# Forming the weighted sum of K with K as the weights: a decode block's backward pass on one Trainium2 core

## The chip, the core and the metric

The kernel runs on one core of one Trainium2 chip. The metric is the device time of one execution in microseconds (us), as the median of several runs. A separate execution was recorded by the hardware profiler; its page and trace are what this document reads.

## What is computed

The reference takes one token (a row `x` of 448 values) through a decode block and returns the output together with the gradients of its inputs. The first half is attention with 16 query heads over 8 cached K/V heads of width 256, so that two query heads share each K/V head (a "group", g = 0 to 7). Only the last W = 4096 of the Sk = 32768 cached positions are used. The second half is a gated feed-forward layer of width 1792.

```python
k = k_cache[:, :, Sk - W:, :]          # repeated for the two heads of a group
scores = einsum("bhqd,bhkd->bhqk", q, k) * Dh ** -0.5
p = softmax(scores)
o = einsum("bhqk,bhkd->bhqd", p, v)
h = x + o.reshape(B, Sq, Hq * Dh) @ wo
out = h + ((g * u) @ w_down)           # g, u: layernorm(h) @ w_gate, @ w_up
# returned: out, and the gradients of x, k_cache, v_cache, wq, wo, w_gate, w_up, w_down
```

The gradients of `k_cache` and `v_cache` have the shape of the whole caches. They are zero outside of the window, and those zeros have to be written too: 8 groups x 28672 positions x 256 values x 2 bytes, for each of the two.

For the gradient of the query the kernel needs, for each head, the weighted sum of K, that is the sum over the 4096 positions of p times the row of K. It is called `kbar`. The change concerns how `kbar` is formed.

## The kernel before

**Zeros.** At the start (lines 57 to 62) a tile of zeros is set on VectorE, and SyncE (SP) issues 16 transfers that copy it to the parts of the two cache gradients outside of the window (`out_2`, `out_3`). They are on SP's own DMA queue, and nothing in the kernel waits for them but its end.

**Everything else goes through GpSimd's (POOL's) DMA queue**, in program order: the loads of K and V windows (`load_window`, line 79), of the weights, and all other outputs. Where the tile scheduler finds that a load's target is still being read, the POOL instruction waits, and whatever is behind it on POOL waits too.

**Storage.** `S` holds eight slots of 128 partitions x 8192 values, each wide enough for one window of one group (128 partitions x T = 32 positions x 256). The tables `K_SLOT` and `V_SLOT` (lines 35 and 36) say which group's K and V lie in which slot; slots are used again, so a load has to wait for the last reader of what lay there.

**First half, per group g** (the loop at line 349). The loop issues the loads of the next groups, then `softmax(g)`, then `scores(g + 1)`, then `moments(g)`.

- `scores` (line 279, through `products` at 260) transposes K on TensorE (line 266), copies the transposes out of PSUM alternately on ScalarE (line 210) and VectorE (line 212), and multiplies by the query (line 271).
- `softmax` (line 283) makes the probabilities, once as f32 (`pf`) and once as bf16 (`pT_all`), both laid out as position on partitions, and 32 x 2 columns (t, head).
- `moments` (line 308) goes over the 32 values of t in pairs. For each t and each of the two heads VectorE forms K times the probability into a small buffer `pk` (line 318; three buffers in turn, each for two values of t). Then TensorE issues, for each t: two matmuls of 512 columns into `MT` (line 322, V as weights, both heads' products `pk` as columns), two matmuls of 2 columns into columns 0 to 3 of `acc` (line 325, V as weights, the two heads' probabilities as columns: the attention output), and four matmuls of 1 column into columns 4 to 7 of `acc` (line 329, the products `pk` as weights, a column of ones as the moving operand). The last four add up the products over the 128 partitions: they are `kbar`. The ends of the group copy `MT` and `acc` out (lines 331 to 335).

After the last group `wo` is applied (its second part is loaded at line 376, and line 383 multiplies), followed by the feed-forward layer forward and backward, the gradient of the attention output (line 435) and of the query (line 453, which uses `Mt` and, through line 456, `kbar`).

**Second half, per group** (the loop at line 560): V is transposed again (line 568), the softmax's gradient is formed, and the gradients of the window's K and V are built as matmuls of 512 columns (line 602), copied out of PSUM (lines 210 and 212) into a staging slot and written by POOL at line 607. Outer products for the weights' gradients are formed between them and written at line 477.

The order of instructions on each engine is not written by hand: a scheduler interleaves `scores(g + 1)` with `moments(g)`, and can reorder loads on POOL.

Of the kernel before, what the change touches and what calls it, by code (L numbers as in the profile page):

```python
# [19 lines left out]
T = 32  # L20
# [20 lines left out]
def kernel(  # L41
# [3 lines left out]
    V_, S_, P_ = nc.vector, nc.scalar, nc.tensor  # L45
# [58 lines left out]
    ones_bf = const.tile([128, 128], bf16)  # L104
# [136 lines left out]
    pT_all = const.tile([128, G, T, 2], bf16)  # L241
# [13 lines left out]
    def pk_buf():  # L255
        k = NB + pk_ctr[0] % NB
        pk_ctr[0] += 1
        return Rt[:, k * 1024:(k + 1) * 1024].rearrange("p (i h d) -> p i h d", i=2, h=2)
# [49 lines left out]
    def moments(g):  # L308

        K, Vv, pf = Kw[g], Vw[g], p_f[g]  # L310
        MT = fps.tile([128, 2, 2 * Dh], f32, tag="MT", name="MT")
        acc = fps.tile([128, 8], f32, tag="acc", name="acc")
        for c in range(T // 2):
            pk = pk_buf()
            for i in range(2):
                t = 2 * c + i
                for h in range(2):
                    V_.tensor_scalar(out=pk[:, i, h, :], in0=K[:, t, :], scalar1=pf[:, t, h:h + 1], scalar2=None, op0=ALU.mult)  # L318
            for i in range(2):
                t = 2 * c + i  # L320
                for hf in range(2):
                    P_.matmul(MT[:, hf, :], lhsT=Vv[:, t, hf * 128:(hf + 1) * 128], rhs=pk[:, i, :, :].rearrange("p h d -> p (h d)"),  # L322
                              start=(t == 0), stop=(t == T - 1))
                for hf in range(2):
                    P_.matmul(acc[:, 2 * hf:2 * hf + 2], lhsT=Vv[:, t, hf * 128:(hf + 1) * 128], rhs=pT_all[:, g, t, :],  # L325
                              start=(t == 0 and hf == 0), stop=(t == T - 1), skip_group_check=True)
                for h in range(2):
                    for dk in range(2):
                        P_.matmul(acc[:, 4 + 2 * h + dk:5 + 2 * h + dk], lhsT=pk[:, i, h, dk * 128:(dk + 1) * 128], rhs=ones_bf[:, 0:1],  # L329
                                  start=False, stop=(t == T - 1), skip_group_check=True)  # L330
        S_.copy(out=Mt[:, g, 0, :], in_=MT[:, 0, :])  # L331
        V_.tensor_copy(out=Mt[:, g, 1, :], in_=MT[:, 1, :])
        V_.tensor_copy(out=oT_f[:, 4 * g:4 * g + 4].rearrange("p (h f) -> p f h", f=2), in_=acc[:, 0:4].rearrange("p (f h) -> p f h", h=2))
        V_.tensor_copy(out=kbar[:, 4 * g:4 * g + 4], in_=acc[:, 4:8])
        V_.tensor_copy(out=oT_bf[:, 4 * g:4 * g + 4], in_=oT_f[:, 4 * g:4 * g + 4])
# [13 lines left out]
    for g in range(G):  # L349
        if g + 1 < NV:  # L350
            load_V(g + 1)
        if g + 2 < 7:
            load_K(g + 2)
        if g == 5:
            load_V(5)
        if g == 6:
            load_V(6)
            load_K(7)
        if g == 7:
            load_V(7)  # L360
            IO.dma_start(out=woA, in_=wo_v[:, 0:16, :])
        softmax(g)
        if g + 1 < G and g != 6:
            scores(g + 1)
        moments(g)
        if g == 6:
            scores(7)
        if g == 0:

            t = ps.tile([128, D], f32, tag="tmp", bufs=1)  # L370
            P_.matmul(t[:], lhsT=ones_bf[0:1, :], rhs=go_bf[:], start=True, stop=True)
            S_.copy(out=dh2_bc[:], in_=t[:])
            for c in range(FC):
                V_.tensor_tensor_reduce(out=wd0[:, c, :], in0=wd0[:, c, :], in1=dh2_bc[:], scale=1.0, scalar=0.0,
                                        op0=ALU.mult, op1=ALU.add, accum_out=d_hh[:, c:c + 1])
# [73 lines left out]
    for h in range(H):  # L449
        for dk in range(2):  # L450
            for hf in range(2):
                c0 = (h % 2) * Dh + dk * 128
                P_.matmul(dq_ps[:, 2 * h + dk:2 * h + dk + 1], lhsT=Mt[:, h // 2, hf, c0:c0 + 128], rhs=doT_f[:, 2 * h + hf:2 * h + hf + 1],  # L453
                          start=(hf == 0), stop=(hf == 1))
# [105 lines left out]
    for g in range(G):  # L560
# [3 lines left out]
        for q in range(8):  # L564
# [6 lines left out]
            for i in range(4):  # L571
                for dh in range(2):
                    P_.matmul(dp[:, 4 * q + i, :], lhsT=xt[:, i, dh, :], rhs=doT[:, 4 * g + dh:4 * g + dh + 3:2],  # L573
                              start=(dh == 0), stop=(dh == 1))
# [22 lines left out]
        for c in range(T // 2):  # L597
            d_ps = bps.tile([128, 2, 2, Dh], f32, tag="d2", bufs=2)
            for i in range(2):
                t = 2 * c + i  # L600
                k, a = t // 8, t % 8
                P_.matmul(d_ps[:, i, :, :].rearrange("p w d -> p (w d)"), lhsT=rows[32 * k:32 * k + 32, a, :], rhs=R[32 * k:32 * k + 32, :],  # L602
                          start=True, stop=True)
# [36 lines left out]
```

## Time and profile before

| | us |
|---|---|
| median of the runs (three, 816.27 to 816.81) | 816.36 |
| the profiled execution, its own time | 816.48 |
| its span in the profile | 814.7 |
| TensorE busy, of the span | 504.1 |
| VectorE busy | 374.4 |
| ScalarE busy | 165.0 |

The span runs from the first to the last instruction or transfer that the profiler saw; 1.78 us of the execution's own time lie around it. In the profile PE is TensorE's matmuls, PEld its weight loads, DVE VectorE, ACT ScalarE, POOL GpSimd, SP SyncE; L329 is line 329. `a<-b` in a row is an operation that writes tile a from tile b, followed by partitions x elements and by the count after an x. A strip of 40 digits gives the busy share of 40 equal slices of the span in tenths (9 is 90% or more); "PEclk" is the clock that TensorE was granted, in tenths of full speed. A matmul's duration overlaps its neighbours', so the spacing of their starts says more about TensorE than the duration.

### The profile page before, as it was taken

How to read it: one execution, taken by the hardware profiler on the slowest of the kernel's cores; microseconds unless marked ns; L12 is line 12 of the kernel's file. 1: busy time of each engine (PE TensorE's matmuls, PEld its weight loads, DVE VectorE, ACT ScalarE, POOL GpSimd, SP SyncE). 2: the span in 40 equal slices, each digit the busy share in tenths (PEclk: the TensorE clock that was granted, in tenths of full speed). 3: DMA queues.
4: the chain of work that ended last, by engine and by line, in shares of the span. 5: the costliest groups of instructions: out<-in, count | busy, mean ns of one | idle time of the engine just before them, and what ended most of it. 6: DMA issues, size and time to landing. Idle time of an engine off the chain costs nothing.

```text
span 814.7 us, 12155 instructions
## 1 busy us (share of the span) xinstructions
PE 504.1 (62%) x4991; PEld 301.7 (37%) x4991; DVE 374.4 (46%) x1149; ACT 165.0 (20%) x261; POOL 40.4 (5%) x75
## 2 busy tenths in 40 slices
PE   3559969999566947062995562597597848263200
PEld 3445646666434524031983421243143313010000
DVE  4128837776451644028733470754553626253200
ACT  0230211221101000001012231243343424142100
POOL 3000000000000001000001000001000010000000
PEclk9959878999785969565556555555555555555555
DMA  8999999999999999999999999999999999999993
GB/s 344 430 423 427 430 428 429 425 428 426 430 417 426 415 424 420 428 429 431 426 427 429 409 415 421 431 423 422 404 430 425 425 413 423 421 425 427 424 427 170
DMA packets 24573, 338.66 MB, mean 416 GB/s; under 512 B 1251, under 2 KB 1317, under 8 KB 4677
## 3 DMA queue, kind: packets, MB, share of 16 engines
q1 hardware_dynamic: 14596, 234.88, 68.3%
q0 software_dynamic: 9920, 103.00, 30.2%
q8 instruction: 39, 0.64, 0.3%
q14 instruction: 18, 0.14, 0.0%
HBM read 57.28 MB, written 280.59 MB: 415 GB/s over the span
## 4 chain that ended last, share of the span: by engine, by line
issue 59%; DMA 17%; PE 11%; DVE 4%; POOL 3%; ACT 1%; POOLq 0%; DVEq 0%
DMA S<-in_A_wo_dram 4%; DMA Rt<-in_A_wq_dram 4%; DMA out_dram<-Mt 3%; PE dq_ps L453 3%; DMA S<-in_A_k_cache_dram 3%; DMA S<-in_A_v_cache_dram 2%; PE MT L322 2%; POOL out_dram L477 1%; POOL S L79 1%; DVE Rt L423 1%; POOL out_dram L607 1%; PE dh_ps L159 1%; PE d_ps L602 1%; PE tr L568 1%; PE t L413 1%
## 5 line engine op out<-in xcount | busy, mean ns | idle before, releaser
L602 PE MATMUL d_ps<-R,Mt 32*128 32x512 bf16 x256 | 124.4, 612 | 94.4 <-DVE S L212 93.6
L322 PE MATMUL MT<-Rt,S 128*128 128x512 bf16 x512 | 156.8, 391 | 21.1 <-DMA S<-in_A_v_cache_dram 19.9
L318 DVE TENSOR_SCALAR Rt<-S,pf 128x256 bf16<-128x256 bf16 x512 | 117.8, 283 | 32.0 <-PE acc L329 17.3
L212 DVE CAST S<-d_ps 128x512 bf16<-128x512 f32 x128 | 86.8, 689 | 57.1 <-ACT S L210 43.9
L210 ACT CAST S<-d_ps 128x512 bf16<-128x512 f32 x128 | 75.1, 587 | 171.6 <-PE d_ps L602 171.6
L266 PE MATMUL tr<-ident_bf,S 128*128 128x128 bf16 x512 | 52.5, 267 | 44.5 <-DMA S<-in_A_k_cache_dram 41.2
L602 PEld LDWEIGHTS <-Mt 32*128 32x128 bf16 x256 | 23.2, 113 | 148.1 <-issue 146.7
L325 PEld LDWEIGHTS <-S 128*128 128x128 bf16 x512 | 49.9, 98 | 62.7 <-issue 6.6
L568 PE MATMUL tr<-ident_bf,S 128*128 128x128 bf16 x512 | 68.8, 304 | 3.5 <-ACT Mt L210 3.5
L329 PE MATMUL acc<-ones_bf,Rt 128*128 128x1 bf16 x1024 | 61.8, 163 | 0.0
L568 PEld LDWEIGHTS <-S 128*128 128x128 bf16 x512 | 48.5, 135 | 28.0 <-issue 27.8
L266 PEld LDWEIGHTS <-S 128*128 128x128 bf16 x512 | 41.4, 121 | 42.9 <-DMA S<-in_A_k_cache_dram 41.7
L210 ACT COPY Rt<-tr 128x1024 bf16<-128x1024 bf16 x32 | 32.4, 1012 | 84.7 <-PE tr L266 84.3
L325 PE MATMUL acc<-pT_all,S 128*128 128x2 bf16 x512 | 49.1, 165 | 0.0
L329 PEld LDWEIGHTS <-Rt 128*128 128x128 bf16 x1024 | 44.5, 96 | 0.0
L212 DVE COPY Rt<-tr 128x1024 bf16<-128x1024 bf16 x32 | 22.1, 690 | 48.5 <-PE tr L266 47.0
L210 ACT COPY Mt<-tr 128x1024 bf16<-128x1024 bf16 x32 | 32.4, 1014 | 56.3 <-PE tr L568 29.2
L322 PEld LDWEIGHTS <-S 128*128 128x128 bf16 x512 | 32.0, 97 | 21.7 <-DMA S<-in_A_v_cache_dram 20.4
L331 ACT COPY Mt<-MT 128x512 f32<-128x512 f32 x8 | 4.7, 586 | 164.8 <-PE MT L322 145.4
L573 PEld LDWEIGHTS <-Mt 128*128 128x128 bf16 x512 | 19.9, 108 | 36.7 <-DVE Mt L212 13.7
L573 PE MATMUL dp<-doT,Mt 128*128 128x2 bf16 x512 | 22.6, 168 | 12.3 <-DVE Mt L212 10.5
L212 DVE COPY Mt<-tr 128x1024 bf16<-128x1024 bf16 x32 | 22.0, 686 | 16.4 <-PE tr L568 11.3
(182 smaller groups left out, 435.1 us busy)
## 6 DMA issues: line engine op xcount, KB each, us to landing
out_dram<-zeros SPq DMA_DIRECT2D x16, 14336.0 KB, 149.7
out_dram<-S POOLq DMA_DIRECT2D x16, 2048.0 KB, 29.5
S<-in_A_v_cache_dram POOLq DMA_DIRECT2D x11, 2048.0 KB, 35.6
S<-in_A_k_cache_dram POOLq DMA_DIRECT2D x8, 2048.0 KB, 28.0
out_dram<-Mt POOLq DMA_DIRECT2D x6, 896.0 KB, 22.3
S<-in_A_wq_dram POOLq DMA_DIRECT2D x1, 3584.0 KB, 14.7
S<-in_A_wo_dram POOLq DMA_DIRECT2D x2, 1792.0 KB, 35.4
out_dram<-Mt POOLq DMA_DIRECT2D x3, 1024.0 KB, 35.7
```

Of the source, the lines that this page charges most:

```text
L79: IO.dma_start(out=dst, in_=cache[0, g, Sk - W:, :].rearrange("(p t) d -> p t d", t=T))
L210: S_.copy(out=out, in_=in_)
L212: V_.tensor_copy(out=out, in_=in_)
L266: P_.transpose(tr[:, i, dh, :], Xw[:, 4 * q + i, dh * 128:(dh + 1) * 128], ident_bf[:])
L318: V_.tensor_scalar(out=pk[:, i, h, :], in0=K[:, t, :], scalar1=pf[:, t, h:h + 1], scalar2=None, op0=ALU.mult)
L322: P_.matmul(MT[:, hf, :], lhsT=Vv[:, t, hf * 128:(hf + 1) * 128], rhs=pk[:, i, :, :].rearrange("p h d -> p (h d)"), start=(t == 0), stop=( ...
L325: P_.matmul(acc[:, 2 * hf:2 * hf + 2], lhsT=Vv[:, t, hf * 128:(hf + 1) * 128], rhs=pT_all[:, g, t, :], start=(t == 0 and hf == 0), stop=(t ...
L329: P_.matmul(acc[:, 4 + 2 * h + dk:5 + 2 * h + dk], lhsT=pk[:, i, h, dk * 128:(dk + 1) * 128], rhs=ones_bf[:, 0:1], start=False, stop=(t == ...
L453: P_.matmul(dq_ps[:, 2 * h + dk:2 * h + dk + 1], lhsT=Mt[:, h // 2, hf, c0:c0 + 128], rhs=doT_f[:, 2 * h + hf:2 * h + hf + 1], start=(hf = ...
L568: P_.transpose(tr[:, i, dh, :], Vw[g][:, 4 * q + i, dh * 128:(dh + 1) * 128], ident_bf[:])
L573: P_.matmul(dp[:, 4 * q + i, :], lhsT=xt[:, i, dh, :], rhs=doT[:, 4 * g + dh:4 * g + dh + 3:2], start=(dh == 0), stop=(dh == 1))
L602: P_.matmul(d_ps[:, i, :, :].rearrange("p w d -> p (w d)"), lhsT=rows[32 * k:32 * k + 32, a, :], rhs=R[32 * k:32 * k + 32, :], start=True, ...
```

## The change

The four matmuls of 1 column become two of 2 columns. The weights are now K's own tile (128 positions x 128 of the 256 columns) instead of the product `pk`, and the moving operand is the two heads' bf16 probabilities instead of a column of ones. The same four columns of `acc` receive the result: columns 4 + dk and 6 + dk.

```diff
@@ moments(g), for each t @@
-                for h in range(2):
-                    for dk in range(2):
-                        P_.matmul(acc[:, 4 + 2 * h + dk:5 + 2 * h + dk], lhsT=pk[:, i, h, dk * 128:(dk + 1) * 128], rhs=ones_bf[:, 0:1],
-                                  start=False, stop=(t == T - 1), skip_group_check=True)
+                for dk in range(2):
+                    P_.matmul(acc[:, 4 + dk:7 + dk:2], lhsT=K[:, t, dk * 128:(dk + 1) * 128], rhs=pT_all[:, g, t, :],
+                              start=False, stop=(t == T - 1), skip_group_check=True)
```

The products `pk` stay: line 322 still needs them. TensorE becomes a reader of K's slot within `moments`, which it was not before.

Over the kernel, 8 groups x 32 values of t x 4 = 1024 matmuls and their weight loads become 512 and 512. On POOL the scheduler puts some loads in another order: for the last groups it issues V6, K7, the first part of `wo`, V7 where it issued K7, V6, V7, the first part of `wo`.

## The prediction, as it was put on record

> **What bounds the kernel now.** I read the page's strips first, since a kernel that writes so much may be held by its transfers.
>
> ```profile
> PE   3559969999566947062995562597597848263200
> PEclk9959878999785969565556555555555555555555
> DMA  8999999999999999999999999999999999999993
> GB/s 344 430 423 427 430 428 429 425 428 426 430 417 426 415 424 420 428 429 431 426 427 429 409 415 421 431 423 422 404 430 425 425 413 423 421 425 427 424 427 170
> DMA packets 24573, 338.66 MB, mean 416 GB/s; under 512 B 1251, under 2 KB 1317, under 8 KB 4677
> ## 3 DMA queue, kind: packets, MB, share of 16 engines
> q1 hardware_dynamic: 14596, 234.88, 68.3%
> q0 software_dynamic: 9920, 103.00, 30.2%
> q8 instruction: 39, 0.64, 0.3%
> ```
>
> The DMA strip is 9 in all slices but the first and the last: the 16 DMA engines have work without a break. TensorE's strip falls to 0 in places, and to 0 at the end. The bytes are set by the outputs: the zeros (SP's queue, q1) are 234.88 MB, POOL's queue (q0) carries 103.00 MB. The slices between the ends move 404 to 431 GB/s; 338.66 MB at 425 are 797 us. So the transfers alone explain the span but for some 18 us at its two ends (814.7 - 797).
>
> Next the end, by windows (columns: PE, PEld, DVE, ACT, POOL busy with counts, PE's clock, DMA share, GB/s), POOL's last instructions, and what was issued there.
>
> ```profile
> 765.00:797.00 32.00, 0.00 (x0) 0.00 (x0) 0.00 (x0) 0.00 (x0) 0.00 (x0) 0.50 1.01 430
> 797.00:815.00 18.00, 0.00 (x0) 0.00 (x0) 0.00 (x0) 0.00 (x0) 0.00 (x0) 0.50 0.30 127
> ```
> ```profile
> 761.91 0.53 POOL L607 DMA_DIRECT2D out_dram<-S  x1 [0.19 <-issue]
> ```
> ```profile
> L607 POOL DMA_DIRECT2D out_dram<-S x16: 532/533/589, 517.1 to 761.9; - x16
> DMA to landing us min/median/max: 17.0/29.5/41.4
> ```
>
> No compute engine does anything after 765, and yet 50 us follow with transfers, 32 of them at full rate. The last output is issued at 761.9; with the longest landing of its kind, 41.4 us, it is there by 803.3, and the span ends at 814.7. What is left by then are the zeros. So **the zeros' queue ends the span**, and POOL's queue only takes a share of engines that are busy anyway. In the last 18 us the engines are 0.30 busy: some finish early, and the last of them sets the end (on average an engine is done 0.70 x 18 = 12.6 us before it).
>
> How late may POOL's work come before it costs anything? From 765 on 430 x 32 + 127 x 18 = 16.0 MB are moved. The two outputs issued at 761.2 and 761.9 are 2048 KB each, 4.2 MB; allowing 0.5 MB for what was still open, zeros for 11.3 MB remain, 26 us at 430 GB/s. Only if the last output were issued over 26 us later would the engines fall idle for want of zeros. That is **the slack of everything on the compute engines**.
>
> **The change, part by part.** The rows for `moments`, in order: its groups on the page, one value of t in the timeline of TensorE, and VectorE beside it in the last group.
>
> ```profile
> L322 PE MATMUL MT<-Rt,S 128*128 128x512 bf16 x512 | 156.8, 391 | 21.1 <-DMA S<-in_A_v_cache_dram 19.9
> L318 DVE TENSOR_SCALAR Rt<-S,pf 128x256 bf16<-128x256 bf16 x512 | 117.8, 283 | 32.0 <-PE acc L329 17.3
> L329 PE MATMUL acc<-ones_bf,Rt 128*128 128x1 bf16 x1024 | 61.8, 163 | 0.0
> L325 PE MATMUL acc<-pT_all,S 128*128 128x2 bf16 x512 | 49.1, 165 | 0.0
> ```
> ```profile
> 304.94 0.59 PE L322 MATMUL MT<-Rt,S 128*128 128x512 bf16 x2
> 305.37 0.19 PE L325 MATMUL acc<-pT_all,S 128*128 128x2 bf16 x2
> 305.43 0.24 PE L329 MATMUL acc<-ones_bf,Rt 128*128 128x1 bf16 x4
> 305.52 0.59 PE L322 MATMUL MT<-Rt,S 128*128 128x512 bf16 x2
> ```
> ```profile
> 301.00 13.28 DVE L318 TENSOR_SCALAR Rt<-S,pf 128x256 bf16<-128x256 bf16 x46 [0.24 <-PE acc L329]
> 317.34 0.16 DVE L333 COPY oT_f<-acc 128x4 f32<-128x4 f32 x1 [3.06 <-PE acc L329]
> ```
>
> *Removed from TensorE.* Four matmuls of 1 column last 0.24 us together and 0.163 each, so they start (0.24 - 0.163) / 3 = 0.026 us apart. A matmul of 2 columns costs the same: 0.165 by its row, and two in 0.19 are again 0.026 apart. So two fewer per t save 0.05 us of 0.58 (305.52 - 304.94); 256 values of t (8 x 32) give 13 us of TensorE's time. Bounds: nothing, if another engine paces `moments`; and 31 us, half of the group's 61.8 us busy. I take what the pace allows: VectorE's products go at 13.28 / 46 = 0.289 us, two for each t: 0.577. TensorE at 0.53 would wait for VectorE at 0.577. Where both run undisturbed the gain is therefore 0.58 - 0.577, under 1 us in all; it is up to 13 us where TensorE also has the next group's transposes in between.
>
> *K's slot is released later.* A load into a slot that held K waited for VectorE's last product; now it waits for TensorE's last matmul as well.
>
> ```profile
> POOL S L79 <- DVE Rt L318: 235.3, 7, 46.6
> ```
> ```profile
> 279.34 0.53 POOL L79 DMA_DIRECT2D S<-in_A_v_cache_dram  x1 [42.70 <-DVE Rt L318]
> 279.94 1.17 POOL L361 DMA_DIRECT2D S<-in_A_wo_dram  x1
> ```
> ```profile
> 279.34 17.70 DMA S<-in_A_v_cache_dram
> 315.17 33.41 DMA S<-in_A_wo_dram
> ```
> ```profile
> S<-in_A_v_cache_dram POOLq DMA_DIRECT2D x11, 2048.0 KB, 35.6
> S<-in_A_wo_dram POOLq DMA_DIRECT2D x2, 1792.0 KB, 35.4
> ```
>
> Seven loads wait so. TensorE ends a group 3.06 us after VectorE (314.28 against 317.34), so each comes up to 3 us later, with all that stands behind it on POOL. Bounds: 0, since K is loaded two groups ahead, and 7 x 3.06 = 21 us if none were hidden; nearer to 0, since of the seven only V7's load is in the chain of waits as a transfer that was waited for (279.34).
>
> *V7 goes behind wo.* V7's load was issued at 279.34, before the first part of `wo`; now it is behind it. It loses about 1.8 us of issue (279.94 + 1.17 - 279.34) and the time in which `wo` is ahead of it on q0. No row shows that. Bounds: 0, and the 35.4 us that `wo` takes to land. The nearest row is V7's own 17.70 us for 2048 KB in the same place: for 1792 KB, 15.5 us. TensorE waits for V7 in the chain, so `moments(7)` and what follows (the second part of `wo`, 33.41 us) move by some 17 us.
>
> *The sum on the work's path*: +17 for V7, 0 to +3 for the slots, -1 to -13 for the matmuls: 4 to 19 us later. I expect the last output at about 775 instead of 762. That is inside the slack of 26 us, and so **costs nothing at the end**; the cover is the zeros, and without them it would cost those 4 to 19 us.
>
> *Fewer instructions to fetch.* This is the one part that touches the DMA engines themselves. Row q8: 39 packets, 0.64 MB, 0.3% of 16 engines x 814.7 us = 39 us, so 1.0 us each (0.84 to 1.17 with the rounding). TensorE has 4991 matmuls and as many loads in this trace, 9982, and 9982 / 39 is 256: q8 fits TensorE's instructions in packets of 256. 1024 fewer are 4 packets, 4 us of one engine's time. Bounds at the end of the span: 4 x 1.17 = 4.7 us if the engine that ends last had carried all four, nothing if it had none, and 1 us to the other side if a fetch falls on it that went elsewhere. I take them spread evenly: 4 / 16 x 1.0 = 0.25 us. [...]
>
> **Sum**: 816.48 (the profiled execution: 814.7 and 1.78 around it) - 0.25 = 816.2 us. The runs' median is 816.36, within 0.02% of that execution. A measurement of this kernel tells about 0.2%, 1.6 us, from no change.
>
> **The rivals.**
>
> *TensorE is the bound after all, and its 13 us come off*: 816.5 - 13 = 803. For it: its strip stands at 9 in many slices of the first half. Against it: the same bytes would have to go at 338.66 MB / (814.7 - 13 - 18) us = 432 GB/s on average between the ends, above every slice of the strip.
>
> *The fetches come off the engine that ends last*: one gives 815.5, two 814.5, all four 812.5. For it: the end is set by single engines (0.30 busy). Against it: the page does not say where q8's packets go, and for four of 16 engines' worth to meet one is unlikely.
>
> *The work's path outruns the slack* (slower): V7 behind `wo` at its upper bound, 35.4 + 1.8, less 1 for the matmuls, is 36 us; 26 are covered, and the other 10 are added at the end, for then POOL's last outputs travel alone: 826.5. It decides from 26 us on. For it: q0's landings are long everywhere (35.6 us median for V's loads). Against it: V7 itself took 17.70 there.
>
> *TensorE's clock falls.*
>
> ```profile
> 40.00:60.00 20.00, 10.43 (x121) 8.98 (x122) 5.78 (x22) 5.91 (x10) 0.00 (x0) 0.53 1.01 428
> 160.00:180.00 20.00, 19.07 (x293) 12.74 (x288) 13.63 (x57) 3.98 (x8) 0.53 (x1) 1.00 1.01 427
> ```
>
> Where it was half busy it was granted 0.53 of its clock, where it was busy 19.07 of 20 us it was granted 1.00. If 10% less work tipped all of `moments` to half, its two long matmuls for each t, 0.59 - 0.376 = 0.213 us apart, would take 0.43 us more together: 256 x 0.43 = 110 us, 84 beyond the slack, 900 us. Against it: at 0.53 of every 0.577 us TensorE stays 92% busy, near the second window's 95%. [...]
>
> That the change does not do what it says is no rival: the built kernel has 512 matmuls and 512 weight loads fewer in TensorE's list.
>
> **How the numbers follow.** Forecast (816.2, end set by the zeros, within 0.6 us either way): 0.80. Fetches off the last engine: 0.12, half of it one fetch (815.5, within 0.2%), half more (faster). TensorE's 13 us: 0.03. Path beyond the slack: 0.04. Clock: 0.01. So faster by over 0.2%: 0.06 + 0.03 = 0.09; slower: 0.05; within: 0.86. The range 814.6 to 817.2 holds the forecast, one fetch or a little over one less (814.6 is just above two), and a fetch more than before with the runs' own scatter; the other cases, some 0.14, are left out.
>
> **What would show it.** The strips of DMA and GB/s unchanged; the last fall of the DMA strip in the same place; q8 at 35 packets. Line 328's new matmuls at about 0.165 us each, 512 of them, and VectorE's wait for `acc` inside `moments` (17.3 us) smaller. POOL's loads at line 79 waiting for TensorE instead of VectorE, V7 landing some 15 us later, and the last output at 766 to 781. The prediction is wrong if the windows after the last output show the engines less than full before the zeros are through, if the span follows the last output's time, or if the end moves although both queues' rates stay.

## The result: 2 us faster, outside the range

| | before | changed |
|---|---|---|
| median of nine runs each, us | 816.45 (816.16 to 816.81) | 814.37 (814.02 to 814.65) |
| span of the profiled execution, us | 814.7 | 812.7 |
| instructions in the trace | 12155 | 10923 |

The ratio is 0.9974, with a 95% interval of 0.9964 to 0.9984: 2.1 us faster, beyond the 0.2% that the prediction took as the bound, and below its range (814.6). The same views again, first the page of the changed kernel.

```profile
span 812.7 us, 10923 instructions
PE   3559949999647519035497576099759674554500
DMA  8999999999999999999999999999999999999994
GB/s 344 427 426 429 427 433 424 432 424 429 431 422 431 418 429 429 409 430 429 427 427 433 423 410 418 430 428 417 424 406 429 424 418 419 420 427 422 427 427 187
q1 hardware_dynamic: 14596, 234.88, 68.4%
q0 software_dynamic: 9920, 103.00, 30.3%
q8 instruction: 35, 0.57, 0.3%
```

The DMA strip has not moved, and q8 is at 35 packets as worked out. The bytes of q0 and q1 are the same. So the kernel still ends with its transfers. The trace has 1232 entries fewer, and not only the 1024 of the prediction: VectorE's waits at semaphores, which stand in it as entries of their own, fell from 487 to 275, and POOL has 4 more. The windows of its last part and POOL's last instruction:

```profile
765.00:797.00 32.00, 2.61 (x6) 0.48 (x4) 2.61 (x4) 1.75 (x3) 1.06 (x2) 0.50 1.00 425
797.00:813.00 16.00, 0.00 (x0) 0.00 (x0) 0.00 (x0) 0.00 (x0) 0.00 (x0) 0.50 0.28 118
```
```profile
769.89 0.53 POOL L606 DMA_DIRECT2D out_dram<-S  x1 [0.19 <-issue]
```

The work's last output is issued 8 us later than before (769.89 against 761.91), and the kernel ends 2 us earlier. Whatever brought the 2 us did not come along the work's path. Inside `moments` TensorE's new pace is the one predicted, 0.53 for each t (310.41 to 310.94):

```profile
310.41 0.59 PE L322 MATMUL MT<-Rt,S 128*128 128x512 bf16 x2
310.84 0.19 PE L325 MATMUL acc<-pT_all,S 128*128 128x2 bf16 x2
310.89 0.19 PE L328 MATMUL acc<-pT_all,S 128*128 128x2 bf16 x2
310.94 0.59 PE L322 MATMUL MT<-Rt,S 128*128 128x512 bf16 x2
```

Where does the time come from, then? Cut the last 16 us of both kernels into short windows. A share of 0.06 is one of 16 engines. Before:

```profile
798.00:803.00 5.00, 0.00 (x0) 0.00 (x0) 0.00 (x0) 0.00 (x0) 0.00 (x0) 0.50 0.64 275
803.00:808.00 5.00, 0.00 (x0) 0.00 (x0) 0.00 (x0) 0.00 (x0) 0.00 (x0) 0.50 0.21 88
808.00:814.00 6.00, 0.00 (x0) 0.00 (x0) 0.00 (x0) 0.00 (x0) 0.00 (x0) 0.50 0.05 22
```

Changed:

```profile
796.00:801.00 5.00, 0.00 (x0) 0.00 (x0) 0.00 (x0) 0.00 (x0) 0.00 (x0) 0.50 0.78 334
801.00:806.00 5.00, 0.00 (x0) 0.00 (x0) 0.00 (x0) 0.00 (x0) 0.00 (x0) 0.50 0.23 98
806.00:812.00 6.00, 0.00 (x0) 0.00 (x0) 0.00 (x0) 0.00 (x0) 0.00 (x0) 0.50 0.06 25
```

In both, **the last 4 to 5 us belong to one single DMA engine** that is still busy with its share of the zeros: in the records one packet of zeros follows another, 0.61 us each, with no other under way, for 5.4 us before and for 4.4 us in the changed kernel. The question is why that one engine is through earlier.

### The profile page after: what moved, and what is told of

Its sections match the earlier page's. It is cut to its first block, busy times and chain, and to the rows that moved or that the text cites. A ratio compares the mean times of both kernels' runs of the same rounds, so it can differ in the third digit from the quotient of the medians.

```text
span 812.7 us, 10923 instructions
## 1 busy us (share of the span) xinstructions
PE 495.5 (61%) x4479; PEld 289.6 (36%) x4479; DVE 374.0 (46%) x1149; ACT 164.7 (20%) x261; POOL 40.5 (5%) x75
## 4 chain that ended last, share of the span: by engine, by line
issue 29%; DMA 16%; PE 11%; DVE 4%; POOL 2%; ACT 1%; POOLq 0%; DVEq 0%
DMA S<-in_A_v_cache_dram 4%; DMA S<-in_A_wo_dram 4%; DMA Rt<-in_A_wq_dram 4%; DMA out_dram<-Mt 3%; PE dq_ps L452 3%; PE MT L322 2%; POOL out_dram L476 1%; DVE Rt L422 1%; POOL out_dram L606 1%; PE dh_ps L159 1%; PE d_ps L601 1%; PE tr L567 1%; PE t L412 1%; PE ao L382 1%; DVE Rt L511 1%
## 5 line engine op out<-in xcount | busy, mean ns | idle before, releaser
L322 PE MATMUL MT<-Rt,S 128*128 128x512 bf16 x512 | 145.9, 397 | 30.7 <-DMA S<-in_A_v_cache_dram 29.8
L318 DVE TENSOR_SCALAR Rt<-S,pf 128x256 bf16<-128x256 bf16 x512 | 117.0, 281 | 56.4 <-PE MT L322 49.7
L567 PE MATMUL tr<-ident_bf,S 128*128 128x128 bf16 x512 | 69.6, 306 | 3.5 <-ACT Mt L210 3.5
L325 PEld LDWEIGHTS <-S 128*128 128x128 bf16 x512 | 49.4, 100 | 60.9 <-issue 9.5
L266 PE MATMUL tr<-ident_bf,S 128*128 128x128 bf16 x512 | 48.6, 253 | 36.4 <-DMA S<-in_A_k_cache_dram 32.0
L567 PEld LDWEIGHTS <-S 128*128 128x128 bf16 x512 | 49.2, 137 | 28.0 <-issue 27.8
L266 PEld LDWEIGHTS <-S 128*128 128x128 bf16 x512 | 38.1, 115 | 34.7 <-DMA S<-in_A_k_cache_dram 32.3
L325 PE MATMUL acc<-pT_all,S 128*128 128x2 bf16 x512 | 48.2, 166 | 0.0
L328 PE MATMUL acc<-pT_all,S 128*128 128x2 bf16 x512 | 47.5, 164 | 0.0
L322 PEld LDWEIGHTS <-S 128*128 128x128 bf16 x512 | 33.5, 98 | 36.7 <-DMA S<-in_A_v_cache_dram 30.7
L210 ACT COPY Mt<-tr 128x1024 bf16<-128x1024 bf16 x32 | 32.4, 1014 | 56.6 <-PE tr L567 29.5
L382 PE MATMUL ao<-S,oT_bf 128*1 128x448 bf16 x32 | 9.6, 468 | 45.9 <-DMA S<-in_A_wo_dram 45.9
L328 PEld LDWEIGHTS <-S 128*128 128x128 bf16 x512 | 30.9, 97 | 0.1
```

What stands on the lines that cost most here:

```text
L210: S_.copy(out=out, in_=in_)
L266: P_.transpose(tr[:, i, dh, :], Xw[:, 4 * q + i, dh * 128:(dh + 1) * 128], ident_bf[:])
L328: P_.matmul(acc[:, 4 + dk:7 + dk:2], lhsT=K[:, t, dk * 128:(dk + 1) * 128], rhs=pT_all[:, g, t, :], start=False, stop=(t == T - 1), skip_g ...
L382: P_.matmul(ao[:], lhsT=oT_bf[:, b:b + 1], rhs=wo_b(b), start=(b == 0), stop=(b == 31))
L567: P_.transpose(tr[:, i, dh, :], Vw[g][:, 4 * q + i, dh * 128:(dh + 1) * 128], ident_bf[:])
```

## The experiments

Theories at the start: **F**, TensorE's instructions come in fewer packets, and those burdened the engine that ends last. **M**, the work's transfers moved and fall differently on that engine. **P**, TensorE's shorter time in `moments`. A fourth, **N**, came up on the way. Every time below is a median over executions; the kernel before, measured beside each, was at 816.3 to 816.6. The interval behind a ratio is its 95% interval.

### Instructions added back, taken away, and transfers put in another order

`a_mid512`: the changed kernel with 1024 instructions added where TensorE idles.

```diff
+    idle = ps.tile([2, 2], f32, tag="tmp", bufs=1, name="idle")
+    for n in range(512):
+        P_.matmul(idle[:], lhsT=oT_bf[:, 28:30], rhs=oT_bf[:, 30:32], start=True, stop=True)
     ao = ps.tile([1, D], f32, tag="tmp", bufs=1)
```

> The changed kernel with 512 matmuls of 2 columns and their 512 weight loads (1024 instructions) added where TensorE waits for the second part of wo; their result is not used. Theory F (the end is set by one DMA engine, and it is done earlier because TensorE's instructions are fetched in fewer packets, 35 instead of 39): the packets are 39 again and the time is back at 816.4 us. Rival M (the order and time of the work's transfers moved by 8 us, and fall differently on the engine that ends last): the order of transfers is that of the changed kernel, so 814.4 us. Rival P (TensorE's shorter time in moments): 814.4 us.

Measured 815.97 us, a ratio to before of 0.9994 (0.9986 to 1.0003): 1.6 of the 2 us are gone again, with `moments` as short as in the changed kernel. Against M and P.

`b_nokbar`: the kernel before without the four matmuls.

```diff
-                for h in range(2):
-                    for dk in range(2):
-                        P_.matmul(acc[:, 4 + 2 * h + dk:5 + 2 * h + dk], lhsT=pk[...], rhs=ones_bf[:, 0:1], ...)
+                if t == 0:
+                    P_.matmul(acc[:, 4:8], lhsT=Vv[:, t, 0:128], rhs=ident_bf[:, 0:4], start=False, stop=True, ...)
```

> The kernel before with the four matmuls of 1 column left out, but for one matmul of 4 columns in each group that only gives the four columns of acc some value: kbar is not formed. About 2030 instructions fewer than before, 8 packets, 31 instead of 39. Theory F: twice the saving of the change, 812.4 us; if only every eighth packet falls on the engine that ends last, one packet's worth, 814.4 to 815.4 us. Rival M: 816.4 us if the transfers keep their order, for K's slot has no new reader. Rival P: four matmuls off instead of two, 812.4 us.

Measured 811.94 us (0.9944, 0.9931 to 0.9956), twice the saving of the change. P foretells the same, so this run speaks against M alone.

`b_half`: the kernel before with those matmuls for one head alone.

```diff
-                for h in range(2):
+                for h in range(1):
```

> The kernel before with the matmuls of 1 column for one of the two heads left out: 512 matmuls and 512 weight loads fewer, the same count as in the changed kernel, while K's slot has no new reader and V7 stays ahead of the first part of wo. kbar of the second head is not formed (the first head's stands in its place). Theory F (number of instruction packets): 35 packets, 814.4 us. Rival M (order and time of the transfers): 816.4 us. Rival P (TensorE's shorter time in moments): 814.4 us.

Measured 814.84 us (0.9982, 0.9973 to 0.9990). Here K's slot has no new reader, V7 stays ahead of `wo`, and the last output is issued at 766.6. So 1.5 of the 2.1 us come without either move of the transfers.

`a_wolate` and `b_wofirst` swap the order of V7 and the first part of `wo`, each against its own kernel.

```diff
+            V_.tensor_copy(out=S[:, 6, 0:1], in_=p_f[7][:, 0, 0:1])   # a_wolate: wo's first load has to wait for softmax(7)
             IO.dma_start(out=woA, in_=wo_v[:, 0:16, :])
...
+            V_.tensor_copy(out=S[:, 5, 0:1], in_=oT_f[:, 27:28])      # b_wofirst: V7's load has to wait for moments(6)
             load_V(7)
```

> The changed kernel, with one VectorE copy of one column into wo's slot ahead of wo's first load, taken from the probabilities of group 7, so that V7 is issued ahead of the first part of wo, as before the change. 35 packets stay. Theory F: 814.4 us. Rival M: 816.4 us. Rival P: 814.4 us.

> The kernel before, with one VectorE copy of one column into V7's slot ahead of V7's load, taken from the result of group 6, so that the first part of wo is issued ahead of V7, as in the changed kernel. 39 packets of instructions stay. Theory F: 816.4 us. Rival M: 814.4 us. Rival P: 816.4 us.

`a_wolate` measured 814.35 us (0.9975, 0.9965 to 0.9985), the changed kernel's time to 0.02. `b_wofirst` measured 818.03 us (1.0019, 1.0010 to 1.0028): not the gain that M wants, and 1.6 us worse than any theory had it. Its last output is late enough to end the kernel (the last packet of the outputs is through at 813.8, the last of the zeros at 810.2):

```profile
782.49 0.53 POOL L608 DMA_DIRECT2D out_dram<-S  x1 [0.19 <-issue]
```
```profile
SPq L636 <- DMA out_dram<-S: 103.6, 2, 100.1
SPq L636 <- DMA out_dram<-zeros: 28.6, 1, 28.6
```

In its waits of SP's queue at the end, 100.1 us are for the work's outputs; before, the longest for them was 66.5 us. So this is the predicted slower rival made real: 20.6 us later than before (782.49 - 761.91) the work's path is past its slack, and the run can't decide on M. M falls by `a_mid512`, `b_half` and `a_wolate`.

### How the time follows the number

`a_mid256` has 256 of the added matmuls in place of 512; `a_both1024` has the 512 and another 512 behind the last group (operands from the last staging slots).

> The changed kernel with 256 unused matmuls and their weight loads (512 instructions, 2 packets: 37) where TensorE waits for the second part of wo. Theory F in its even form (each packet costs the engine that ends last 0.4 to 0.5 us, as 35, 39 and 31 packets have it so far): 815.2 us. Theory F in steps (one packet in eight, or two, fall on that engine): 814.4 or 815.9 us, nothing between. Rivals M and P: 814.4 us.

> The changed kernel with 512 unused matmuls and loads in the wait for wo and 512 more behind the last product of the last group (2048 instructions, 8 packets: 43). Theory F, even: 814.4 + 8 x 0.45 = 818.0 us. In steps, with two packets of eight on the last engine: 817 us. Rivals M and P: 814.4 us, for the work's transfers keep their order and moments is as short as in the changed kernel.

Measured 815.11 us (0.9984, 0.9975 to 0.9993) and 818.39 us (1.0026, 1.0016 to 1.0036): close to the even form of F, and 815.11 is not one of the steps. The points so far, by the number of instructions in each trace (without `b_wofirst`, which its outputs end):

| kernel | instructions | q8 packets | median us |
|---|---|---|---|
| b_nokbar | 9892 | 31 | 811.94 |
| a_wolate | 10889 | 35 | 814.35 |
| changed | 10923 | 35 | 814.37 |
| b_half | 10990 | 35 | 814.84 |
| a_mid256 | 11401 | 37 | 815.11 |
| a_mid512 | 11913 | 39 | 815.97 |
| before | 12155 | 39 | 816.45 |
| a_both1024 | 12937 | 43 | 818.39 |

The line through them rises by 2.0 ns for each instruction, and no point is over 0.5 us from it. (Some traces lack up to 35 records of matmuls; with these counted in, the slope is the same.) The end of `a_both1024`, in windows:

```profile
800.00:805.00 5.00, 0.00 (x0) 0.00 (x0) 0.00 (x0) 0.00 (x0) 0.00 (x0) 0.50 0.39 167
805.00:810.00 5.00, 0.00 (x0) 0.00 (x0) 0.00 (x0) 0.00 (x0) 0.00 (x0) 0.50 0.06 26
810.00:816.00 6.00, 0.00 (x0) 0.00 (x0) 0.00 (x0) 0.00 (x0) 0.00 (x0) 0.50 0.05 22
```

and of `b_nokbar`:

```profile
794.00:799.00 5.00, 0.00 (x0) 0.00 (x0) 0.00 (x0) 0.00 (x0) 0.00 (x0) 0.50 0.81 347
799.00:804.00 5.00, 0.00 (x0) 0.00 (x0) 0.00 (x0) 0.00 (x0) 0.00 (x0) 0.50 0.31 134
804.00:810.00 6.00, 0.00 (x0) 0.00 (x0) 0.00 (x0) 0.00 (x0) 0.00 (x0) 0.50 0.11 46
```

With more instructions one engine is alone for some 9 us (0.06 and 0.05 from 805 on); with fewer, the last window stands at 0.11, 1.8 engines on average. The others did not get later in `a_both1024`: its share is at 0.06 from 805 to 810, where the kernel before has 0.21 from 803 to 808. More packets of instructions on q8 should have delayed the engines that carry them, and F says that the last one is among them. On which engines they run is not shown, and packets and instructions rise together in the table, so that it can't tell one from the other. That gives theory **N**: not the packets but the instructions themselves, of whatever engine, hold up the engine that ends last, by the line's 2 ns each. How they would is not shown.

### Instructions of other engines

`a_other896` and `a_other640` leave TensorE's list alone and add copies on VectorE and ScalarE. The second has 128 and 64 of them at the end in place of 320 and 128.

```diff
+    for n in range(320):
+        V_.tensor_copy(out=idle_v[:], in_=oT_bf[0:2, 30:32])
+    for n in range(128):
+        S_.copy(out=idle_s[0:2, :], in_=oT_bf[0:2, 30:32])
     ao = ps.tile([1, D], f32, tag="tmp", bufs=1)
```

The same two loops stand behind the last group once more, reading the last staging slot.

> The changed kernel with 640 copies of 2x2 values on VectorE and 256 on ScalarE whose results are not used, half of them in the wait for the second part of wo and half behind the last group; TensorE's instructions stay (35 packets on q8). Theory F (TensorE's packets on q8 set it): 814.4 us. Theory N (every instruction, of whatever engine, delays the packets of one DMA engine by about 2 ns, and that engine ends last; 11 points of time against the trace's instruction count lie on 2.1 ns each): 814.4 + 896 x 0.0021 = 816.3 us. Rival P (TensorE's time): 814.4 us.

> The run before with fewer additions at the end, so that they are through before the zeros are: the changed kernel with 320 copies of 2x2 values on VectorE and 128 on ScalarE in the wait for the second part of wo, and 128 and 64 behind the last group, results not used; q8 stays at 35 packets. Theory N (every instruction of any engine delays one DMA engine, 2.1 ns by the points so far): 814.4 + 640 x 0.0021 = 815.7 us; with 3 ns for an instruction of ScalarE or VectorE 816.3 us. Theory F (TensorE's fetch packets) and rival P (TensorE's time): 814.4 us.

`a_other896` measured 832.09 us (1.0191, 1.0177 to 1.0205) and its time tells nothing of its question: the copies at the end took 157 ns each and outlasted the transfers. In its window there is no transfer left while VectorE (the third number) still works:

```profile
812.00:829.00 17.00, 0.00 (x0) 0.00 (x0) 13.86 (x89) 0.00 (x0) 0.00 (x0) 0.50 0.00 1
```

Its transfers do tell something: the last packet of zeros is through at 813.1 us, against 811.1 in the changed kernel, 2 us later, near what N has.

`a_other640` measured 816.13 us (0.9995, 0.9986 to 1.0004). In its page and its last windows:

```profile
span 814.9 us, 11541 instructions
q8 instruction: 35, 0.57, 0.3%
q14 instruction: 20, 0.16, 0.0%
```
```profile
803.00:808.00 5.00, 0.00 (x0) 0.00 (x0) 0.00 (x0) 0.00 (x0) 0.00 (x0) 0.50 0.17 72
808.00:814.00 6.00, 0.00 (x0) 0.00 (x0) 0.00 (x0) 0.00 (x0) 0.00 (x0) 0.50 0.05 22
```

q8 is at 35 packets, every compute engine was done by 794, and one engine again ends alone. The median is 1.8 us above the changed kernel's: 618 instructions more in the trace, 2.8 ns each. One rival is close to F: the page has a second queue with packets of instructions, q14, and counts 20 there where the changed kernel's page has 16. One takes 0.31 us in the records of the changed kernel, so that even if all four fell on the engine that ends last they would cost it 1.2 of the 1.8 us. F and P, which had 814.4, don't explain it, N stands; why these instructions cost more than the 2.0 ns of the line is open.

`a_tt` tried to use this: VectorE's products of a pair of t by one instruction instead of four.

```diff
-                for h in range(2):
-                    V_.tensor_scalar(out=pk[:, i, h, :], in0=K[:, t, :], scalar1=pf[:, t, h:h + 1], scalar2=None, op0=ALU.mult)
+            V_.tensor_tensor(out=pk, in0=K[:, 2 * c:2 * c + 2, :].unsqueeze(2).to_broadcast([128, 2, 2, Dh]),
+                             in1=pf[:, 2 * c:2 * c + 2, :].unsqueeze(3).to_broadcast([128, 2, 2, Dh]), op=ALU.mult)
```

> The changed kernel with VectorE's four products of a pair of t formed by one instruction of 1024 columns instead of four of 256: 128 instructions instead of 512, the same values and about the same VectorE time. Theory N: 384 fewer instructions, and fewer of VectorE's waits, of which there are 410 at that line in the profile before; 384 to 700 x 0.0021 = 0.8 to 1.5 us less, 812.9 to 813.6 us. Theory F and rival P: 814.4 us.

Measured 820.77 us (1.0051, 1.0039 to 1.0064). VectorE's time was not "about the same":

```profile
L315 DVE TENSOR_TENSOR Rt<-S,pf 128x1024 bf16<-128x1024 bf16 x128 | 149.7, 1221 | 84.4 <-PE MT L320 83.8
```
```profile
781.00:797.00 16.00, 8.51 (x20) 2.08 (x19) 7.02 (x11) 5.26 (x9) 1.60 (x3) 0.50 0.76 316
```

One takes 1221 ns where four took 4 x 281. The work's path grew until the DMA engines ran out of zeros while outputs were still being formed (share 0.76; the last packet of zeros is through at 785.4, the last of the outputs at 816.9). Again the slower rival, not a test of N.

### The share of the last engine

Four kernels tried to take rows of zeros off the engine that ends last, by splitting the last fill of zeros alone into transfers from fewer partitions, which were meant to leave engines out. The edit of `a_k15`:

```diff
-            FILL.dma_start(out=reg, in_=zeros[:].unsqueeze(1).to_broadcast([128, NZ, ZW]))
+                FILL.dma_start(out=rows[0:768, :].rearrange("(p n) f -> p n f", p=128), in_=zeros[0:128, :].unsqueeze(1).to_broadcast([128, 6, ZW]))
+                FILL.dma_start(out=rows[768:888, :].rearrange("(p n) f -> p n f", p=120), in_=zeros[0:120, :].unsqueeze(1).to_broadcast([120, 1, ZW]))
+                FILL.dma_start(out=rows[888:896, :].rearrange("(p n) f -> p n f", p=8), in_=zeros[0:8, :].unsqueeze(1).to_broadcast([8, 1, ZW]))
```

`a_k12` has 108 and 20 rows, from as many partitions, in place of 120 and 8. `a_f15` reads the 120 rows from 15 partitions, 8 times each. `a_f8` sends 832 rows from 64 partitions and 64 from 8.

> The changed kernel; of the last of the 16 transfers of zeros 120 of 896 rows are issued over 15 partitions and 8 over 8 partitions, so that if a transfer over 15 partitions leaves out one DMA engine, that one has 7 to 8 rows (of 16 KB, 0.61 us each by their share of the page) less, 4.5 us, and the others half a row more. Theory F says that a single engine sets the end; if it is the one left out, the span ends 3 to 4 us earlier, 810.5 to 811.5 us, held by the next engines; if it is another, 814.7 us. If all engines end together, contrary to F, 814.7 us.

> The changed kernel; of the last transfer of zeros 64 of 896 rows are issued over 8 partitions, so that if such a transfer uses 8 engines, those have 4 rows more and the other 8 have 4 rows less, 2.4 us each way. Theory F (a single engine sets the end): 2.4 us later (816.8 us) if it is among the first eight, up to 2.4 us earlier (812.0 us) if it is among the others and the first eight have room. If the engines end together: 816.8 us.

> [...]

> [...]

Measured 824.58, 860.03, 819.44 and 824.02 us: all slower than the changed kernel's 814.37, the first two by more than the split was to cost. In `a_f8` the transfers themselves become slow: its strip falls to 326 GB/s in slice 35 and to 235 to 269 in slices 36 to 39.

```profile
GB/s 349 429 426 426 428 433 426 426 428 430 427 424 422 420 431 413 426 432 427 429 431 410 422 419 428 419 423 408 429 427 422 416 421 424 326 235 269 257 269 96
```

`a_k15` and `a_k12` are later than the changed kernel by 5.1 and 9.7 us, about the time of 8 and 16 rows at 0.61 us. That the last engine got more rows instead of fewer is an estimate from these two times; which engine it is, and how such a split is dealt out, is not shown. The try failed, and none of the kernels here that form all results beats the changed one.

## Why the prediction was wrong

**What held.** The transfers bound the kernel and the zeros end it: all the views agree. TensorE's saving of 0.05 us for each t is there (0.53 instead of 0.58), and no gain came from it: with the same `moments`, `a_mid512` is back near the old time. V7 behind `wo` cost 18.6 us on the way, 15.5 foretold:

```profile
267.73 36.30 DMA S<-in_A_v_cache_dram
```

36.30 us to land instead of 17.70, and in `a_wolate`, where V7 goes ahead of `wo` again, it is 17.93. But V7 was issued at 267.73 instead of 279.34, and what brought that is not what the prediction had. By the end of group 5 the shorter matmuls, with all else, had won 4 us (VectorE copies that group's `acc` at 231.9 instead of 235.9). The other 8 came in group 6, whose V6 is now loaded ahead of K7:

```profile
233.18 0.53 POOL L79 DMA_DIRECT2D S<-in_A_k_cache_dram  x1 [35.44 <-DVE Rt L318]
236.12 0.53 POOL L79 DMA_DIRECT2D S<-in_A_v_cache_dram  x1 [2.41 <-PE mt L288]
```
```profile
232.16 0.53 POOL L79 DMA_DIRECT2D S<-in_A_v_cache_dram  x1 [35.73 <-PE acc L328]
232.75 0.53 POOL L79 DMA_DIRECT2D S<-in_A_k_cache_dram  x1
```

The first pair is from before. TensorE's first matmul with V6 starts at 261.06 before and at 248.93 in the changed kernel. The prediction has no term for this swap, and no run tested it by itself. So 18.6 us lost at V7 and 11.6 won ahead of it leave V7 landing 7 us later, not 15. The last output came 8 us later, inside the 4 to 19 (the swap, which the sum did not have, helped), and cost nothing, as the cover said. One sign was misjudged on the way: VectorE's wait inside `moments` became longer, not shorter.

```profile
L318 DVE TENSOR_SCALAR Rt<-S,pf 128x256 bf16<-128x256 bf16 x512 | 117.0, 281 | 56.4 <-PE MT L322 49.7
```

It is idle there for 56.4 us instead of 32.0. Of the 49.7 us behind TensorE's line 322 one wait is 22.1 us long, in which TensorE waits for V7, and VectorE for the buffers that TensorE holds. The prediction's last sign of being wrong, an end that moves although both queues' rates stay, is what came.

**What failed.** The step "Fewer instructions to fetch". It was the right place, the one term that touched the DMA engines, and the right sign; its price was 0.25 us and it measured 2.1. The average over 16 engines ("I take them spread evenly") was the wrong reading of an end which the last window, 0.30 busy, already showed to be uneven: what counts is the engine that ends last, alone for 5.4 us. The mechanism was not borne out either: in `a_other640` the end moved by 1.8 us with q8 at 35 packets as in the changed kernel. 1232 fewer in the trace x 2.0 = 2.5 us by the line of the table, 2.1 measured; what path the 2.0 ns take no row of the page shows. Of the 1232 the prediction counted 1024 and priced only their fetching; that an instruction which runs could cost more than that was put at nothing. The rival "the fetches come off the engine that ends last" had 814.5 for two packets; that this is near the measured time does not bear it out, for fetches on q8 do not explain `a_other640`.

**Where else it was off.** The slack was taken as 26 us. `b_wofirst`, 20.6 us late, is already past it: the last output, issued at 782.49, shares the engines with the zeros until 810.2 and is through at 813.8, 31 us after its issue (the median before was 29.5), instead of travelling alone at full rate.

**What stays open.** Why the end moves by 2 ns for an instruction. Whether the profiler's recording has a part in it is not shown: each timed run here has a span and a clock, so each was recorded, and a run without records was not made. If it has, the gain may be one of recorded executions alone. That the end moves by 1.3 to 2.8 ns for each instruction that is added or left out is shown, for TensorE's by themselves and for VectorE's and ScalarE's together; by what path is not.

## What to carry to other kernels

In a kernel that its transfers bound, look at the last windows first. Here the DMA share fell to 0.05, about 1 of 16, and a single engine set the end, alone for 5.4 us; the cost had to be asked of that engine, not of the average of 16. Even instructions far off the critical path had a price here, 2.0 us for each thousand (in executions that the profiler records), so that fewer instructions gained where a shorter `moments` by itself did not (`a_mid512`, 815.97 us). And a cover has an end: the two kernels that went past it, `b_wofirst` (818.03 us) and `a_tt` (820.77 us), lost more than the count of instructions could give.

## What the hardware showed unexpectedly

- The end of the kernel moved by about 2 ns (2.0 by the line through eight kernels, 1.3 to 2.8 by single runs) for each instruction that TensorE, or VectorE and ScalarE, ran, while one DMA engine alone was still busy at the end (5.4 us before, 4.4 us in the changed kernel).
- In the records a packet of instructions on q8 takes 0.94 us, where a packet of zeros of the same 16 KB takes 0.61.
- A last fill of zeros with 832 rows read from 64 partitions and 64 rows from 8 (`a_f8`, not tried one by one) brought the rate from about 425 down to 235 to 269 GB/s.
- One VectorE product of 1024 columns with two broadcast operands took 1221 ns, where four of 256 columns with a scalar operand took 281 each.
